# A transformer block on one core: three loads issued behind the copies into the query ring, at the last two attention units, and one rounding of the output weights later in ScalarE's list

## Chip, core and metric

The kernel runs on one core of a Trainium2 chip. The metric is the device time of one execution in microseconds (us). TensorE (PE, with its weight loads as PEld), VectorE (DVE), ScalarE (ACT), GpSimd (POOL) and SyncE (SP, which here only issues DMAs) each work through a list of instructions in order and wait for each other through semaphores.

## What is computed

One block with conditioning (adaLN), sliding-window attention over 2048 tokens with 32 heads of width 16, and a gated FFN, all in float32:

```python
mod = (_silu(c) @ w_mod).reshape(c.shape[0], 6, 1, -1)
sa, ca, ga, sb, cb, gb = (mod[:, 0], mod[:, 1], mod[:, 2], mod[:, 3], mod[:, 4], mod[:, 5])
h = _layernorm(x, axis=-1) * (1 + ca) + sa
x = x + ga * _A_ref(h, A_wqkv, A_wo)       # H = 32, Dh = 16, window of 256 keys
h = _layernorm(x, axis=-1) * (1 + cb) + sb
x = x + gb * _B_ref(h, B_w1, B_w3, B_w2)   # silu(h w1) * (h w3), then w2; F = 1792
```

```python
mask = (idx[:, None] - idx[None, :] >= 0) & (idx[:, None] - idx[None, :] < W)
scores = jnp.where(mask[None, None], scores, -1e9)
p = _softmax(scores, axis=-1)
```

## The kernel before

Products that need more than TensorE's rounded float32 (`F32R`) are made from two parts: a tile is rounded by ScalarE, and VectorE or GpSimd subtracts the rounded part from the tile to get the rest; three products of parts are summed. "Rounding" and "split" below are these two steps.

**Attention** runs in 32 units, one for each group of 4 heads (8 groups) and block of 512 tokens (4 blocks). A unit passes three stages, which for different units lie beside each other in time.

- `unit_a`: the products for queries and keys (L560), rounding and split, and DMAs that place the rows in two tiles that are kept, `ringk` and `ringq` (L579, L581).
- `unit_b`: 16 products of scores (L607, tile `mx`), of each the row maximum over the window on VectorE (L616, into `mt`); the maxima are turned (L622), rounded on ScalarE with the sign changed (`mT`, L626), the rest made on VectorE (L629), and both parts are copied by two DMAs of 8 KB each into two further rows of `ringq` (L633). So a product with `ringq` then subtracts the maximum by itself. These are "the copies" below, two for each unit.
- `unit_c`: the scores again, with the maxima in them (L925, tile `st`, three banks of PSUM), then either a copy (L930), masks on GpSimd (L935) and the exponential (L946), or a merge of two blocks on VectorE (L952), the exponential on ScalarE (L962) and masks on GpSimd; the products with the values (L975, `po`); the result is copied (L982, `os`) and stored (L985, `o_dr`).

**The output projection** starts while the last units still run. Its weights come from `wog` in four loads of 256 KB (L1215), each with a rounding on ScalarE (L1136) and a split on GpSimd or VectorE (L1137). The sums of the softmax are loaded, inverted (`reciprocal`, L1240, between loads L1236 and stores L1241 to `r_dr`); attention's results and the inverses come back in loads of 256 KB each (L1260 from `o_dr`, L1255 from `r_dr`), are multiplied (L1269), rounded (L1264) and split (L1272), and multiplied with the weights (L1283). The input `x` is loaded again in tiles of 256 KB (L1221, `x1a`, `x1b`) and the projection is added to it on VectorE with the sums for the second layernorm (L1153). The FFN follows (L1542, L1638) to the end.

**The order.** From the last units on, the order of all work is a table of numbers, `ORDER`. A negative number is a step of attention, the others are steps of the later phases; the program issues the steps in this order, and each engine gets its instructions, and SyncE its DMAs, in the order in which they come up. An engine whose next instruction waits holds up all that stands behind it on that engine, and this holds for SyncE's queue too. The steps that matter here are -3364 and -3365 (the copies of the last unit but one), -3477 and -3478 (those of the last unit), 14 (the rounding of the second quarter of the output weights), 42 and 43 (loads L1260 and L1255 for the first quarter of the first block), 24 and 26 (loads of `x1a`), 16 and 19 (the loads of the third and fourth quarter of the output weights). Semaphores are set by what the steps read and write, so they follow any order.

```python
    if ORDER:
        order = [ids[i] if i < 0 else sch.ops[i].fn for i in ORDER]
...
    with tc.manual_schedule():
        for fn in first + order:
            fn()
```

Of the kernel before, what the change touches and what calls it, by code (L numbers as in the profile page):

```python
# [272 lines left out]
def us(t):  # L273
# [33 lines left out]
    -3172, -3079, -3329, -3178, -3351, -3359, -3077, -3173, -3330, -3179, -3352, -3360, 31, -3181, -3056, -3076,  # L307
    -3331, -3345, -3164, -3343, -3168, -3075, -3332, -3346, -3344, -3432, 10, 33, -3433, -3252, -3434, -3251,
    -3438, -3435, -3440, -3436, -3439, 32, -3437, -3441, -3175, -3165, -3078, -3357, -3333, -3182, -3335, -3264,
    -3358, -3169, 11, -3081, -3183, -3153, -3170, -3159, -3149, -3180, -3174, 12, -3166, -3334, -3336, -3260,  # L310
    -3265, -3341, -3266, -3189, -3353, -3347, -3261, -3342, -3267, -3354, -3263, -3269, -3150, -3348, -3270,
    -3349, -3258, -3253, -3254, -3355, -3337, -3188, -3350, -3271, -3356, -3338, 34, -3186, -3361, -3255, -3259,
    -3273, -3171, -3362, -3167, -3288, -3284, -3452, -3289, -3290, -3442, 6, 7, 8, 9, -3363, -3285, -3453,
    -3291, -3443, -3082, 13, 42, 43, 26, -3364, -3365, -3287, 14, -3293, -3464, -3185, -3184, -3187, -3472,
    -3274, -3444, -3275, -3465, -3473, -3445, -3458, -3456, -3262, -3272, -3256, -3292, -3459, -3457, -3280,
    -3470, -3294, -3279, -3446, -3295, -3448, -3276, -3190, -3281, -3296, -3471, -3447, -3449, -3454, -3377,
    -3373, -3466, -3378, -3379, -3460, -3302, -3455, -3374, -3380, -3467, -3376, -3462, -3383, -3371, -3468,
    -3268, -3282, -3286, -3277, 44, 15, -3375, -3461, -3450, -3382, -3257, -3283, -3278, -3463, -3469, -3451,
    -3384, -3301, -3299, -3474, -3366, -3367, -3298, -3475, -3372, -3368, -3386, -3401, -3402, -3397, -3403,
    -3297, -3300, 2, -3476, -3398, -3404, -3387, 45, -3400, -3406, 48, 47, -3191, 35, 52, 24, 36, 19, 16, 53,  # L320
    -3477, -3478, -3393, -3392, -3407, -3408, -3388, -3303, -3394, -3389, -3409, -3385, -3369, -3381, -3395,
    -3405, -3390, -3399, 54, 49, 46, 37, 87, -3490, -3491, -3486, 94, -3492, -3487, -3493, -3370, -3489, -3495,
    50, -3391, 80, -3496, -3484, -3415, -3414, -3412, -3479, -3480, -3497, -3499, -3485, -3396, -3481, 55,
    -3514, -3515, -3510, -3411, -3410, -3413, -3516, -3085, 22, -3304, 75, 28, 72, 58, 57, 38, 108, 63, 3, 51,
    73, -3511, -3517, 56, 59, -3513, 17, -3519, 95, 101, 81, -3500, -3506, -3520, -3521, -3505, -3501, -3507,
    -3416, 60, -3522, -3502, 68, 74, 25, 62, 67, 157, 76, -3482, -3498, -3518, -3488, -3508, -3512, -3494,
    -3503, 20, -3509, -3483, -3504, 18, 109, 64, 69, 61, 77, 21, 4, 110, -3417, 23, 29, 39, 162, 156, 88, 89,
    102, 96, 82, -3528, -3527, -3525, -3524, -3523, -3526, 65, -3529, 78, 70, 153, -3530, 79, 137, 116, 103,
    104, 90, 97, 123, 83, 5, 40, 105, 84, 85, 106, 91, 98, 154, 92, 71, 66, 1, 255, 262, 111, 112, 166, 256,
    161, 167, 41, 155, 265, 99, 113, 158, 86, 159, 263, 107, 114, 93, 100, 115, 268, 168, 160, 163, 269, 257,  # L330
    164, 169, 207, 27, 171, 204, 172, 208, 117, 138, 130, 131, 118, 124, 132, 139, 133, 125, 126, 140, 119, 176,
    270, 141, 120, 142, 121, 127, 134, 135, 205, 258, 128, 165, 170, 144, 273, 272, 266, 274, 122, 136, 271,
    143, 129, 183, 197, 198, 184, 190, 191, 192, 282, 288, 199, 185, 177, 267, 275, 209, 212, 213, 206, 147,
    218, 146, 217, 148, 173, 276, 283, 174, 290, 210, 289, 175, 277, 214, 223, 151, 150, 222, 145, 496, 152,
    259, 278, 279, 280, 281, 215, 178, 200, 193, 186, 179, 308, 284, 286, 285, 287, 194, 201, 195, 292, 202,
    293, 187, 188, 294, 180, 211, 291, 219, 216, 220, 196, 297, 309, 306, 299, 295, 316, 189, 203, 300, 181,
    307, 296, 298, 303, 221, 224, 234, 248, 227, 235, 241, 242, 249, 228, 243, 229, 312, 314, 310, 250, 236,
    301, 225, 313, 311, 304, 260, 226, 302, 305, 318, 319, 320, 317, 323, 332, 499, 182, 325, 315, 321, 497,
    327, 251, 237, 230, 244, 359, 447, 335, 341, 149, 448, 454, 457, 451, 252, 324, 264, 403, 326, 253, 336,
    337, 238, 239, 342, 328, 245, 231, 246, 333, 261, 322, 343, 329, 240, 360, 254, 363, 377, 361, 365, 367,  # L340
    364, 330, 458, 404, 338, 366, 362, 405, 344, 369, 345, 331, 247, 452, 406, 378, 368, 408, 449, 407, 409,
    383, 374, 371, 385, 381, 379, 410, 500, 339, 372, 453, 386, 375, 232, 373, 376, 233, 395, 382, 370, 455,
    411, 380, 525, 384, 450, 498, 387, 462, 464, 413, 389, 392, 419, 416, 334, 340, 572, 346, 569, 353, 347,
    412, 388, 456, 390, 391, 526, 348, 527, 459, 393, 394, 401, 465, 414, 422, 415, 478, 460, 466, 529, 531,
    461, 528, 573, 417, 530, 570, 397, 399, 354, 355, 349, 467, 402, 350, 463, 482, 472, 475, 484, 468, 532,
    473, 356, 470, 351, 476, 400, 357, 396, 398, 574, 578, 418, 575, 479, 420, 358, 686, 421, 469, 471, 474,
    483, 576, 477, 687, 533, 541, 535, 480, 507, 490, 352, 683, 429, 534, 423, 536, 481, 577, 571, 485, 491,
    488, 424, 425, 688, 508, 492, 537, 585, 486, 501, 538, 493, 515, 503, 579, 539, 489, 430, 431, 432, 433,
    580, 516, 494, 487, 502, 504, 513, 505, 587, 511, 581, 509, 646, 774, 540, 647, 689, 648, 542, 517, 582,
    523, 519, 586, 649, 651, 588, 495, 514, 426, 654, 512, 427, 510, 605, 589, 593, 583, 599, 596, 603, 434,  # L350
    543, 692, 650, 653, 652, 428, 617, 655, 760, 761, 441, 435, 521, 620, 618, 684, 518, 584, 524, 619, 522,
    520, 591, 594, 656, 685, 442, 436, 597, 621, 592, 600, 590, 595, 690, 604, 693, 598, 701, 607, 622, 601,
    611, 626, 437, 602, 623, 443, 444, 438, 763, 606, 439, 445, 506, 694, 699, 624, 609, 612, 608, 613, 627,
    783, 544, 762, 657, 440, 764, 786, 446, 545, 780, 767, 628, 634, 614, 695, 640, 700, 787, 638, 781, 784,
    696, 610, 765, 768, 641, 625, 546, 629, 635, 639, 547, 770, 702, 632, 636, 630, 707, 697, 703, 548, 637,
    615, 691, 616, 785, 631, 698, 710, 551, 789, 769, 644, 549, 782, 788, 552, 708, 642, 704, 771, 731, 550,
    766, 705, 709, 633, 553, 643, 713, 554, 790, 555, 645, 556, 791, 715, 714, 711, 706, 717, 712, 732, 557,
    716, 734, 733, 719, 563, 718, 860, 735, 721, 720, 558, 725, 559, 722, 560, 561, 723, 728, 562, 658, 861,
    564, 726, 736, 565, 566, 724, 567, 862, 738, 727, 659, 568, 729, 740, 730, 737, 792, 739, 741, 742, 793,
    857, 794, 863, 752, 743, 660, 661, 754, 753, 662, 744, 665, 663, 866, 755, 664, 796, 858, 745, 859, 795,  # L360
    746, 864, 797, 798, 666, 747, 667, 668, 867, 669, 800, 865, 799, 670, 671, 748, 801, 802, 804, 749, 868,
    750, 805, 806, 807, 751, 828, 756, 672, 673, 758, 757, 674, 810, 675, 937, 676, 759, 677, 812, 811, 808,
    803, 814, 809, 829, 813, 831, 830, 816, 938, 815, 832, 818, 817, 678, 869, 679, 819, 680, 681, 820, 772,
    822, 870, 682, 939, 821, 825, 773, 823, 833, 824, 826, 835, 827, 834, 837, 836, 839, 934, 838, 940, 943,
    871, 849, 840, 775, 777, 851, 850, 841, 776, 935, 852, 873, 936, 842, 941, 872, 843, 874, 942, 944, 875,
    844, 778, 877, 876, 945, 779, 845, 878, 881, 846, 879, 847, 1011, 882, 884, 853, 848, 905, 855, 854, 887,
    883, 1014, 856, 1012, 889, 1013, 888, 885, 880, 891, 886, 906, 890, 908, 907, 893, 1015, 892, 909, 895, 894,
# [1414 lines left out]
```

## Time and profile before

| | us |
|---|---|
| three runs | 909.71, 909.88, 911.14 (median 909.88) |
| the profiled execution | 910.79, of which its span is 909.0 |
| TensorE busy in the span | 891.9 |
| VectorE, ScalarE, GpSimd busy | 656.7, 525.8, 555.6 |
| mean granted TensorE clock | 0.994 |

The first attention unit's copies are issued at 75.1 us of the span and the last unit's at 413.7; the FFN's first products (L1542) start at 478.8. A row of the timeline gives start, duration, engine, line, operation, tiles (written <- read), shapes and count, and in brackets how long the engine stood idle before it and for whom; SPq is SyncE's queue, where the duration is that of issuing a DMA. A row of busy times by stretch gives the stretch, its length, the busy time and count of PE, PEld, DVE, ACT and POOL, the granted clock, the share of time in which the DMA engines were busy, and what they moved in GB/s. A wait is attributed by semaphore events, to the one that came last.

### The profile page before, as it was taken

To read this page: it belongs to the slowest core of one execution; us is meant where nothing else is said; L and a number is where in the kernel's file an instruction comes from. 1 tells how busy PE (TensorE), PEld (TensorE's weight loads), DVE (VectorE), ACT (ScalarE), POOL (GpSimd) and SP (SyncE) were. 2 spreads that over 40 slices of the span, in tenths; PEclk is the share of its full clock that TensorE was granted. 3 is DMA by queue.
4 is the path that set the end of the run, shared out by engine and by line. 5 is a ranking of instruction groups with operands and counts; after the bars stand their busy time and mean duration, and the time that the engine had idled before them with its cause. 6 is when DMAs were issued, how large, how long until landed. Compare 5 with 4: busy or idle time off the path is not lost.

```text
span 909.0 us, 18284 instructions
## 1 busy us (share of the span) xinstructions
PE 891.9 (98%) x6011; PEld 726.7 (80%) x6011; DVE 656.7 (72%) x1795; ACT 525.8 (58%) x984; POOL 555.6 (61%) x798
## 2 busy tenths in 40 slices
PE   9999999999999999989999999999999999999998
PEld 5777888887888888857777888888888888888886
DVE  6885888877787878775778768757567665565655
ACT  6437787786778787757588734343374334342330
POOL 3126887787878787866577157886579355434220
PEclk9999999999999999988999999999999999999999
DMA  9524556656655566567866677565272523231102
GB/s 304 185 82 121 144 154 179 161 166 172 186 155 160 154 172 170 151 185 213 257 213 202 202 235 265 169 221 162 63 266 64 172 65 105 74 95 40 47 24 93
DMA packets 126238, 141.98 MB, mean 156 GB/s; under 512 B 61112, under 2 KB 73920, under 8 KB 126144
## 3 DMA queue, kind: packets, MB, share of 16 engines
q1 hardware_dynamic: 126000, 140.82, 51.0%
q8 instruction: 47, 0.77, 0.4%
q14 instruction: 47, 0.39, 0.2%
q10 hardware_dynamic: 144, 0.00, 0.0%
HBM read 85.99 MB, written 34.61 MB: 133 GB/s over the span
## 4 chain that ended last, share of the span: by engine, by line
PE 85%; DVE 4%; DMA 1%; ACT 1%; issue 1%; POOL 1%; SPq 0%; POOLq 0%; DVEq 0%; ACTq 0%
PE st L1542 11%; PE mx L1542 10%; PE st L925 9%; PE po L975 9%; PE pj L560 9%; PE mx L607 8%; PE mx L1638 7%; PE st L1638 6%; PE pj L1542 4%; PE po L1542 3%; PE po L1638 2%; PE pj L1638 2%; PE mx L1283 2%; DMA ringq<-mT 1%; PE st L813 1%
## 5 line engine op out<-in xcount | busy, mean ns | idle before, releaser
L616 DVE CUSTOM_DVE_ANT_0 junk<-mx,mskq 128x320 bf16<-128x320 f32 (+4 forms) x512 | 216.4, 466 | 50.9 <-PE mx L607 49.0
L935 POOL TENSOR_SCALAR_AFFINE_SELECT pt<-pt 128x256 f32<-128x256 f32 x472 | 184.2, 412 | 54.1 <-ACT pt L930 24.4
L607 PE MATMUL mx<-ringk,ringq 96*128 96x320 f32 (+4 forms) x512 | 150.1, 315 | 0.3 <-DMA ringq<-qk 0.2
L560 PE MATMUL pj<-hT,wq 128*128 128x512 f32 x384 | 138.9, 401 | 0.0
L962 ACT ACTIVATE pt<-st 128x512 f32<-128x512 f32 (+1 forms) x216 | 117.3, 572 | 32.6 <-DVE st L952 27.6
L925 PE MATMUL st<-ringq,ringk 98*128 98x256 f32 (+1 forms) x536 | 129.7, 331 | 4.2 <-DMA ringq<-mT 2.1
L1137 POOL TENSOR_TENSOR w<-w,w 128x512 fp32r<-128x512 f32 (+2 forms) x49 | 85.6, 1761 | 52.2 <-ACT w L1136 52.2
L607 PEld LDWEIGHTS mx<-ringk,ringq 96*128 96x128 f32 x512 | 96.4, 191 | 12.3 <-DVE mt L616 1.6
L925 PEld LDWEIGHTS st<-ringq,ringk 98*128 98x128 f32 x536 | 88.8, 192 | 15.3 <-ACT pt L962 4.0
L975 PE MATMUL po<-pt,vS 128*17 128x128 f32 (+1 forms) x2144 | 88.5, 313 | 0.3 <-ACT pt L946 0.3
L560 PEld LDWEIGHTS pj<-hT,wq 128*128 128x128 f32 x384 | 71.8, 190 | 10.3
L975 PEld LDWEIGHTS po<-pt,vS 128*17 128x17 f32 x2144 | 60.8, 98 | 22.4 <-issue 5.0
L952 DVE COPY_PREDICATED st<-later,st 128x256 f32<-128x256 uint8 x152 | 62.1, 426 | 22.0 <-PE st L925 19.9
L1589 POOL TENSOR_TENSOR t<-t,t 128x512 f32<-128x512 f32 x25 | 33.6, 1344 | 65.1 <-DVE t L1577 65.1
L1542 PE MATMUL st<-b,w 128*128 128x512 f32 x270 | 66.9, 390 | 0.2 <-DVE x1a L1643 0.2
L1542 PEld LDWEIGHTS st<-b,w 128*128 128x128 f32 x270 | 50.6, 188 | 11.1 <-DVE x1a L1643 0.7
L946 ACT ACTIVATE pt<-pt 128x512 f32<-128x512 f32 (+1 forms) x96 | 52.5, 587 | 10.6 <-POOL pt L935 10.6
L930 ACT ACTIVATE pt<-st 128x512 f32<-128x512 f32 (+1 forms) x96 | 52.0, 545 | 9.1 <-PE st L925 8.4
L1136 ACT ACTIVATE w<-w 128x512 fp32r<-128x512 f32 (+2 forms) x56 | 42.3, 783 | 17.0 <-DMA w<-wraw 12.0
L1577 DVE TENSOR_TENSOR t<-mx,t 128x512 f32<-128x512 f32 x44 | 30.2, 686 | 28.5 <-PE mx L1542 11.6
L573 POOL TENSOR_TENSOR qk<-qkr,qk 128x512 fp32r<-128x512 f32 x32 | 41.1, 1284 | 14.2 <-ACT qk L569 14.0
L813 PE MATMUL st<-wvh,hT 128*128 128x512 f32 x128 | 44.8, 406 | 1.0 <-DVE hT L474 0.8
(326 smaller groups left out, 1888.5 us busy)
## 6 DMA issues: line engine op xcount, KB each, us to landing
ringq<-qk SPq DMA_DIRECT2D x192, 64.0 KB, 2.1
ringk<-qk SPq DMA_DIRECT2D x96, 128.0 KB, 2.4
o_dr<-os SPq DMA_DIRECT2D x32, 256.0 KB, 2.8
w<-wsum SPq DMA_DIRECT2D x14, 512.0 KB, 4.6
w<-w2g SPq DMA_DIRECT2D x14, 512.0 KB, 4.5
jb<-in_w SPq DMA_DIRECT2D x24, 256.0 KB, 4.9
w<-wraw SPq DMA_DIRECT2D x14, 384.0 KB, 3.8
e<-in_w SPq DMA_DIRECT2D x18, 256.0 KB, 3.1
```

What stands on the lines that cost most here:

```text
L560: nc.tensor.matmul(v["ps"], WQ[g][w][:, n // 3], hTp(i, n // 3, b * BT, BT), start=(n == 0), stop=(n == 3 * KC - 1))
L607: nc.tensor.matmul(v[i][:, :n], both_queries(a, gs), keys(NS, a, (gs + 1) * HP - n, n), start=True, stop=True)
L616: nc.vector.tensor_tensor_reduce(out=junk[:, :n], in0=v[i][:, :n], in1=mskq[:, WK - n:], scale=1.0, scalar=-3e38, op0=ALU.add, op1=ALU.max ...
L813: nc.tensor.matmul(v["ps"], hTp(w, k, t * P, P), i[:, k], start=(n == 0), stop=(n == 3 * KC - 1))
L925: nc.tensor.matmul(piece(v[a, k], a, k, m), keys(NM, a, kb * P, P), queries(a, 4 * b + q, n), start=new, stop=not new or len(here(a, k)) = ...
L935: nc.gpsimd.affine_select(out=out, in_=in_, **w)
L952: nc.vector.copy_predicated(o, later, block(v[a, fk], a, fk, m))
L962: nc.scalar.activation(o, i, AF.Exp, scale=SCALE)
L975: nc.tensor.matmul(po[32 * i:32 * i + DH + 1, q * P:(q + n) * P], vS[:, 4 * b + j, 4 * g + i], piece(pt_of(a, k), a, k, m)[:, h], start=i ...
L1137: either(lambda e: e.tensor_tensor(out=lo(), in0=src(), in1=hi().bitcast(F32), op=ALU.subtract), 0.85, 0.06 + 0.0024 * n, key, kl + kh, kl ...
L1542: nc.tensor.matmul(ps(bk), WT[s, n][w][:, col], BB[t, k][r], start=start and c == 0, stop=stop and c == 5, skip_group_check=True)
L1638: nc.tensor.matmul(ps(bk), tiles[hk + (h,)][:, i * P:(i + 1) * P], w2_of(last, y, f), start=(m == 0), stop=(m == 5))
```

## The change

Only `ORDER` differs. Three loads (42, 43, 26) go behind the copies of the last unit but one, the rounding 14 goes 31 places down the table, and three loads (24, 19, 16) go behind the copies of the last unit. The table is laid out anew over more lines, so that every line below it has a number higher by 3: L633 of before is L636 of the change, and so on. The lines of the table that carry the moves:

```diff
-    -3291, -3443, -3082, 13, 42, 43, 26, -3364, -3365, -3287, 14, -3293, -3464, -3185, -3184, -3187, -3472,
...
-    -3297, -3300, 2, -3476, -3398, -3404, -3387, 45, -3400, -3406, 48, 47, -3191, 35, 52, 24, 36, 19, 16, 53,
-    -3477, -3478, -3393, -3392, -3407, -3408, -3388, -3303, -3394, -3389, -3409, -3385, -3369, -3381, -3395,
...
+    7, 8, 9, -3363, -3285, -3453, -3291, -3443, -3082, 13, -3364, -3365, 42, 43, 26, -3287, -3293, -3464,
...
+    -3292, -3459, -3457, -3280, -3470, -3294, -3279, -3446, -3295, -3448, -3276, -3190, -3281, -3296, 14,
...
+    48, 47, -3191, 35, 52, 36, 53, -3477, -3478, 24, 19, 16, -3393, -3392, -3407, -3408, -3388, -3303,
```

On SyncE, at the copies of the last unit but one, the queue before the change reads (the two copies are the row with `ringq<-mT`; the store and the load of output weights stand ahead of everything here):

```order
L985 DMA o_dr_75<-os 128x512
L1215 DMA wo_7326<-wog 128x512
L1260 DMA qkr<-o_dr_72 128x1x512
L1255 DMA qk_7599<-r_dr_77 128x1x512
L1221 DMA x1a<-in_x 128x512
L633 DMA ringq<-mT 1x16x128 x2
L1255 DMA qk_7818<-r_dr_77 128x1x512
```

and of the change:

```order
L988 DMA o_dr_75<-os 128x512
L1218 DMA wo_7326<-wog 128x512
L636 DMA ringq<-mT 1x16x128 x2
L1263 DMA qkr<-o_dr_72 128x1x512
L1258 DMA qk_7601<-r_dr_77 128x1x512
L1224 DMA x1a<-in_x 128x512
L1258 DMA qk_7818<-r_dr_77 128x1x512
```

The copies have passed three loads of 256 KB; what stands ahead of and behind the six is as it was.

On SyncE, at the copies of the last unit, before the change:

```order
L1260 DMA wq_7824<-o_dr_72 128x1x512
L1221 DMA x1a<-in_x 128x512
L1236 DMA wqr<-o_dr_74 96x1x128
L1215 DMA wo_7326<-wog 128x512 x2
L1255 DMA wq_7830<-r_dr_77 128x1x512
L633 DMA ringq<-mT 1x16x128 x2
L1044 DMA wsum<-jb_7174 128x512
```

and of the change:

```order
L1263 DMA wq_7824<-o_dr_72 128x1x512
L1239 DMA wqr<-o_dr_74 96x1x128
L1258 DMA wq_7827<-r_dr_77 128x1x512
L636 DMA ringq<-mT 1x16x128 x2
L1224 DMA x1a<-in_x 128x512
L1218 DMA wo_7326<-wog 128x512 x2
L1047 DMA wsum<-jb_7174 128x512
```

One load of `x` and two of output weights stood ahead of the copies and now stand right behind them.

On ScalarE, between the two units' `mT`, before the change (the rounding of output weights is the row with `wo`):

```order
L946 ACTIVATE pt<-pt 128x256
L962 ACTIVATE pt<-st 128x512
L1136 ACTIVATE wo_7325<-wo_7326 128x512
L962 ACTIVATE pt<-st 128x512
L930 ACTIVATE pt<-st 128x512
L982 ACTIVATE os<-po 128x512
L930 ACTIVATE pt<-st 128x512
L962 ACTIVATE pt<-st 128x512 x3
```

and of the change:

```order
L949 ACTIVATE pt<-pt 128x256
L965 ACTIVATE pt<-st 128x512 x2
L933 ACTIVATE pt<-st 128x512
L985 ACTIVATE os<-po 128x512
L933 ACTIVATE pt<-st 128x512
L965 ACTIVATE pt<-st 128x512
L1139 ACTIVATE wo_7325<-wo_7326 128x512
L965 ACTIVATE pt<-st 128x512 x2
```

Five activations of attention have passed the rounding. TensorE's, VectorE's and GpSimd's lists hold the same instructions in the same order as before.

197 rows, old and new, of the table ORDER are left out of this document.

## The prediction

> **What bounds the kernel now.** The page comes first: TensorE is busy for 98% of the span and carries 85% of the chain that ended last, so only two things on TensorE can move the time: idle time on the chain, and the clock.
>
> ```profile
> span 909.0 us, 18284 instructions
> PE   9999999999999999989999999999999999999998
> PEclk9999999999999999988999999999999999999999
> PE 85%; DVE 4%; DMA 1%; ACT 1%; issue 1%; POOL 1%; SPq 0%; POOLq 0%; DVEq 0%; ACTq 0%
> ```
>
> The clock digit dips in slices 18 and 19 of 40 (386 to 432 us), and the busy digit of TensorE in slice 18. TensorE's waits, asked next, begin with two reasons whose longest cases lie there:
>
> ```profile
> PE st L925 <- DMA ringq<-mT: 2.1, 2, 1.8
> PE st L925 <- ACT pt L962: 2.0, 2, 1.3
> PE st L1283 <- DVE o L1272: 1.8, 1, 1.8
> ```
>
> The columns are total us, times, longest; the third is a wait in the output projection, behind the change. The timeline of TensorE shows both longest ones, 1.26 and 1.78 us, within five microseconds of each other, in the scores of the last two attention units (the x2 row at 406.16 uses the maxima that the copies bring):
>
> ```profile
> 402.98 0.50 PE L925 MATMUL st<-ringq,ringk 98*128 98x256 f32 x2 [1.26 <-ACT pt L962]
> 406.16 0.98 PE L925 MATMUL st<-ringq,ringk 98*128 98x256 f32 x2 [1.78 <-DMA ringq<-mT]
> ```
>
> Busy time by stretch, cut where the clock changes (length, busy PE, PEld, DVE, ACT, POOL, clock, DMA share, GB/s), shows the price behind them:
>
> ```profile
> 400.10:403.51 3.41, 2.15 (x12) 1.53 (x12) 2.40 (x12) 1.69 (x4) 0.44 (x2) 1.00 0.87 244
> 403.51:406.93 3.42, 1.64 (x6) 1.19 (x6) 1.39 (x6) 1.37 (x3) 3.28 (x9) 0.50 0.92 274
> 406.93:410.34 3.41, 3.41 (x20) 2.30 (x19) 2.04 (x8) 2.15 (x5) 3.30 (x5) 0.50 0.75 235
> 410.34:413.75 3.41, 3.41 (x22) 1.44 (x21) 1.32 (x8) 0.79 (x3) 0.00 (x0) 0.50 0.37 130
> 444.47:447.88 3.41, 2.37 (x10) 1.33 (x9) 2.71 (x4) 2.55 (x6) 1.55 (x2) 1.00 0.86 258
> 475.19:478.60 3.41, 2.20 (x10) 1.83 (x11) 3.38 (x6) 2.00 (x3) 1.17 (x1) 1.00 0.17 66
> ```
>
> After a stretch with 2.15 us busy of 3.41 the clock halves, and it comes back only after 10.24 us. TensorE is busy for 1.64+3.41+3.41 = 8.46 us of these; at full clock that is 4.23.
>
> **Part 1: the copies ahead of three loads.** The issuing queue before the change, and one step of the chain of waits:
>
> ```profile
> 396.28 0.55 SPq L985 DMA_DIRECT2D o_dr<-os  x1
> 396.88 0.45 SPq L1215 DMA_DIRECT2D wo<-wog  x1
> 397.37 0.56 SPq L1260 DMA_DIRECT2D qkr<-o_dr  x1
> 398.04 0.55 SPq L1255 DMA_DIRECT2D qk<-r_dr  x1
> 398.63 0.59 SPq L1221 DMA_DIRECT2D x1a<-in_x  x1
> 399.26 1.20 SPq L633 DMA_DIRECT2D ringq<-mT  x2
> 399.88 6.14 DMA ringq<-mT
> DMA to landing us min/median/max: 1.8/1.8/6.1
> 397.77 0.22 DVE L629 SCALAR_TENSOR_TENSOR mT<-mx,mT 16x128 fp32r<-16x128 f32 x1
> ```
>
> The second 8 KB copy takes 6.14 us from issue to landing, where the median of these copies is 1.8. VectorE made its data at 397.77+0.22 = 397.99. So it can be issued at about 398.3 instead of 399.88. The store and the wo load still stand ahead; ScalarE's row below shows that load landed by 401.82, so the copy lands between 400.1 (398.3+1.8) and about 402.2. TensorE, without the 1.26 us, asks for it at 406.16-1.26-1.78 = 403.1. The 1.78 us wait goes.
>
> The price is on the queue: SyncE now waits at the second copy until 397.99, with the three loads and all later ones behind it, and issues the loads at about 399.2 instead of 397.37. The first taker is GpSimd's multiplication L1269.
>
> ```profile
> 403.00 3.98 POOL L935 TENSOR_SCALAR_AFFINE_SELECT pt<-pt 128x256 f32<-128x256 f32 x10 [3.76 <-ACT pt L962]
> 406.95 1.28 POOL L1269 TENSOR_TENSOR qkr<-qkr,qk 128x512 f32<-128x512 f32 x1
> 401.82 0.63 ACT L1136 ACTIVATE wo<-wo 128x512 fp32r<-128x512 f32 x1 [2.30 <-DMA wo<-wog]
> 402.35 0.58 ACT L962 ACTIVATE pt<-st 128x512 f32<-128x512 f32 x1
> 399.21 0.42 DVE L952 COPY_PREDICATED st<-later,st 128x256 f32<-128x256 uint8 x1
> ```
>
> GpSimd's ten masks will start at about 400.4 (part 2) and end at 404.4. With the worst landing seen, 6.14 us, the loads are there at 405.3. So the new wait costs GpSimd from nothing to 0.9 us, and TensorE nothing, as the masks that TensorE needs next stand ahead of L1269. If that cover went, 0.9 us would reach TensorE.
>
> **Part 2: the rounding behind five activations.** L1136 sat for 2.30 us on its load, and the exponential L962 behind it, whose input VectorE had finished at 399.21+0.42 = 399.63, ran at 402.35. It moves to about 399.7, GpSimd's masks with it, and TensorE's 1.26 us wait for L962 goes. The rounding itself then runs at about 403 with its load landed; its taker, GpSimd's split L1137, stands behind L1269, so it is hidden.
>
> **The engine bound of both.** In the 10.24 us at half clock TensorE needs 4.23 at full clock. VectorE is next:
>
> ```profile
> 403.51:413.75 10.24, 4.75 (x20) 0.50 0.68 213
> ```
>
> (VectorE alone: 4.75 us busy.) So this stretch can shrink to 4.75: 10.24-4.75 = 5.49, and with the 1.26 us before it 6.75 us. By TensorE alone it would be 10.24-4.23+1.26 = 7.27.
>
> **Part 3: three loads behind the last unit's copies.** One x1a and two wo loads leave the queue ahead of the last copies, where the queue had time, and come right behind them.
>
> ```profile
> 413.74 1.18 SPq L633 DMA_DIRECT2D ringq<-mT  x2
> 424.52 0.66 ACT L1136 ACTIVATE wo<-wo 128x512 fp32r<-128x512 f32 x1
> 422.59 0.94 DVE L1240 RECIPROCAL mT<-mT 32x128 f32<-32x128 f32 x1 [0.49 <-DMA mT<-o_dr]
> ```
>
> Their own takers have room: the first is the rounding L1136 at 424.52, over 10 us behind the copies at 413.74, and x1a is taken later, with the projection's sums. The edit's own saving is nothing here: the copies of the last unit had an empty queue already, and TensorE shows no wait for them. What they do is load the wire at its tightest: the reciprocal L1240 already waits for its load, and merges for TensorE stand behind it on VectorE. The DMA stretches:
>
> ```profile
> 399.90:402.00 2.10, 1.83 (x10) 1.20 (x8) 2.10 (x11) 0.18 (x1) 0.00 (x0) 1.00 0.99 277
> 402.00:406.00 4.00, 1.39 (x6) 1.00 (x6) 1.88 (x10) 2.88 (x6) 2.80 (x8) 0.69 0.86 254
> 406.00:409.60 3.60, 3.44 (x19) 2.37 (x20) 1.60 (x6) 1.41 (x3) 3.60 (x6) 0.50 0.78 238
> 409.60:412.20 2.60, 2.60 (x17) 1.56 (x20) 1.67 (x7) 1.23 (x3) 0.63 (x2) 0.50 0.66 225
> 412.20:415.60 3.40, 3.40 (x35) 1.59 (x27) 0.79 (x3) 2.11 (x6) 0.45 (x2) 0.77 0.03 10
> 415.60:422.50 6.90, 6.90 (x83) 5.11 (x83) 4.87 (x8) 6.51 (x13) 6.70 (x14) 1.00 0.84 239
> ```
>
> Up to this load 0.58+1.02+0.86+0.59+0.03+1.65 = 4.73 MB pass in 22.6 us, the moved loads among them in both kernels. At 277 GB/s, the rate with the engines full, they need 17.1 us, so the load can land 5.5 us earlier; at 254, 18.6 us and 4.0 earlier. I take 277, since in the changed kernel the idle 3.4 us at 412 fills up and the DMA engines run full.
>
> **Sum.** The engines allow 6.75 us, the wire 5.5; the smaller holds. From it I take 0.3 for two more hand-offs (0.14 us lie between the copy's landing, 399.88+6.14 = 406.02, and the matmul at 406.16). Gain 5.2 us. After that stretch the chain stays on TensorE to the end, with 1.8 us (at L1283) as its longest wait, and what that wait hangs on comes from attention and moves with it, so I let all of the gain arrive. The profiled execution took 910.79 us (span 909.0 and 1.8 around it) and would take 905.6; the median of the runs is 0.91 lower, so 909.88-5.2 = **904.7**. With the wire at 254 GB/s 906.2, with the engines' bound 903.1, with TensorE's own 902.6.
>
> **Rivals.**
> *The clock halves all the same.* For it: stretches with 2.20 and 2.37 us busy kept the clock, one with 2.15 lost it, so the edge is thin, and the new TensorE may still be paced by VectorE there. Against it: the filled 1.26 us lifts that stretch well over 2.4 busy, and no other slice of the page shows a clock under 9 tenths. Then only the waits go: 1.26+1.78-0.3 = 2.7 us, 907.2.
> The Trainium skill (TensorE: Matmul & The Clock Gate, HAM oscillation — how this bites in real kernels) asks only that TensorE have no idle gap above some 3.4 us; by that rule gaps of 1.26 and 1.78 us did not cost the clock, and removing them would not save it: this rival. The trace speaks against the rule, as the clock fell without a gap over 1.78 us.
>
> *The wire gives less.* At 238 GB/s 4.73 MB take 19.9 us, the load comes 2.7 us earlier, and later loads, such as the one that VectorE waits 1.40 us for in the row below, give some back: gain 1.5 to 2.7, 907.2 to 908.4. For it: rows of 225 to 254 GB/s, though with the queue not full. Against it: 277 where it is.
>
> ```profile
> 431.36 0.72 DVE L1269 TENSOR_TENSOR wq<-wq,wq 128x512 f32<-128x512 f32 x1 [1.40 <-DMA wq<-o_dr]
> ```
>
> *It doesn't do what it says.* The copies still stand behind a 256 KB store and a 256 KB load; if they land after 405, the wait and the clock stay: 909.9. Against it: the wo load had landed by 401.82 with three loads behind it.
>
> *Slower.* At the reciprocal L1240 the three loads (0.79 MB, 3.3 us at 238 GB/s) come ahead of its load; VectorE stands, merges behind it, then TensorE. From a stop of 1.26 us in one 3.41 us stretch the clock falls as above, which costs 1.26 to 3.3 and 8.46-4.23 = 4.23 us, so 5.5 to 7.5 against the 5.2 gained: 910.2 to 912.2. For it: L1240 waits already. Against it: the loads come when the wire was idle.
>
> **Numbers.** Forecast 0.56, clock 0.17, wire 0.14, nothing 0.06, slower 0.07. About 0.2% (1.8 us) is what a measurement can tell from no change; the wire's case lies within it with 0.02 of its 0.14. So faster 0.85, same 0.08, slower 0.07. The range reaches from 902.6 (TensorE's own bound) to 908.4 (the wire's low end) and leaves out the last two cases, 0.13.
>
> **What would show it.** Right: no clock of 0.50 around 403 to 414; L633 at about 2 us to landing; the 1.26 and 1.78 gone from TensorE's waits; L962 ahead of L1136 without 2.30 idle; the 412 us hole in the DMA closed; VectorE's wait at L1240 for mT<-o_dr above 0.49. Wrong: the clock at 0.50 there or further on, a wait of TensorE on L952's merges or on L1137 and L1269, or a copy that lands after 403.

## The result, and the profile after

| | before | change |
|---|---|---|
| median of the runs, us | 910.21 (4 runs, 909.71 to 911.14) | 905.38 (4 runs, 904.83 to 907.24) |
| profiled execution / its span, us | 910.79 / 909.0 | 905.31 / 903.5 |
| ratio, 95% interval | | 0.9945 (0.9928 to 0.9962) |

The change takes 4.8 us off the median. The profiled executions lie 5.5 us apart, and about 0.4 of these is not the change's: the turn of the last unit but one (the `mx<-ident,mt` row that makes its `mT`) stands at 397.04 before and at 396.66 after, ahead of everything that was moved. The trace therefore shows some 5.1 us, where the prediction said 5.2. Measured twice more, on two chips, the change took 4.0 and 3.9 us off the median (the table below), so 5 us is the upper end of what was measured. Three executions far above the others of their kernels (975.64, 979.55 and 1458.08 us) are left out of every median and ratio here.

The page of the change, the lines that answer to those of before:

```profile
span 903.5 us, 18286 instructions
PE   8999999999999999999999999999999999999998
PEclk9999999999999999999999999999999999999999
PE 84%; DVE 3%; DMA 2%; ACT 1%; POOL 1%; issue 1%; SPq 1%; POOLq 0%; DVEq 0%; ACTq 0%
```

The clock's two digits of 8 are gone, and so is TensorE's in slice 18. The wait for the copy and the 1.26 us case have left the list of TensorE's waits between 380 and 500 us (us in total, times, longest):

```profile
PE st L1286 <- DVE o L1275: 1.9, 1, 1.9
PE pj L1545 <- DVE b L1443: 1.3, 1, 1.3
PE st L1419 <- ACT wqr L1405: 1.2, 1, 1.2
PE st L928 <- ACT pt L965: 1.0, 2, 0.5
```

Behind the attention's end stand waits that before had too or that come and go between runs. The line with L965 (L962 of before) is new in its place: two waits of half a microsecond at 420.65 and 421.66, to which the section on the steps comes back.

The timeline of both kernels gives the turns of the last two units, first before, then after:

```profile
397.04 0.28 PE L622 MATMUL mx<-ident,mt 128*16 128x128 f32 x1
413.03 0.38 PE L622 MATMUL mx<-ident,mt 128*16 128x128 f32 x1
```

```profile
396.66 0.28 PE L625 MATMUL mx<-ident,mt 128*16 128x128 f32 x1
406.22 0.28 PE L625 MATMUL mx<-ident,mt 128*16 128x128 f32 x1
```

They lie 15.99 us apart before and 9.56 after: 6.43 us are won between them, within 0.02 of the engines' bound of 6.75 less 0.3. (In the two later profiles of the change they lie 9.64 and 9.60 us apart, so the agreement is closer than the profiles agree with each other.) The distance between these two rows serves below as the measure of the place; it doesn't contain what happens earlier in a run. The busy times of the change by stretch show what ends it now (length, busy PE, PEld, DVE, ACT, POOL, clock, DMA share, GB/s):

```profile
400.10:403.51 3.41, 3.41 (x22) 2.45 (x24) 3.41 (x17) 2.69 (x5) 2.52 (x8) 1.00 0.86 252
403.51:406.93 3.42, 3.42 (x47) 2.04 (x48) 3.00 (x14) 3.03 (x7) 3.42 (x5) 1.00 0.99 300
406.93:410.34 3.41, 3.41 (x55) 2.38 (x46) 2.34 (x5) 3.36 (x8) 3.15 (x8) 1.00 0.55 157
412.20:415.60 3.40, 3.40 (x38) 2.26 (x37) 1.58 (x4) 3.03 (x8) 3.26 (x7) 1.00 1.01 375
```

TensorE has no idle time left here, the clock is whole, and VectorE is busy for 3.41 of 3.41 and 3.00 of 3.42 us: the engine that the prediction named as next. Both engines are full here, so that VectorE and not TensorE sets the pace is argued and not shown. The DMA hole of before at 412 is filled (1.01 of the time busy, 375 GB/s).

### The profile page after: what moved, and what is told of

Same layout as the page of the kernel before. It is cut to its first block, busy times and chain, and to the rows that moved or that the text cites. A ratio compares the mean times of both kernels' runs of the same rounds, so it can differ in the third digit from the quotient of the medians.

```text
span 903.5 us, 18286 instructions
## 1 busy us (share of the span) xinstructions
PE 887.5 (98%) x6011; PEld 723.5 (80%) x6011; DVE 654.2 (72%) x1795; ACT 526.2 (58%) x984; POOL 555.4 (61%) x798
## 4 chain that ended last, share of the span: by engine, by line
PE 84%; DVE 3%; DMA 2%; ACT 1%; POOL 1%; issue 1%; SPq 1%; POOLq 0%; DVEq 0%; ACTq 0%
PE st L1545 11%; PE mx L1545 10%; PE st L928 9%; PE po L978 9%; PE pj L563 9%; PE mx L610 8%; PE mx L1641 7%; PE st L1641 6%; PE pj L1545 4%; PE po L1545 3%; PE po L1641 2%; PE pj L1641 2%; PE st L816 1%; DVE b L1443 1%; POOL xt L747 1%
## 5 line engine op out<-in xcount | busy, mean ns | idle before, releaser
L965 ACT ACTIVATE pt<-st 128x512 f32<-128x512 f32 (+1 forms) x216 | 117.2, 572 | 33.3 <-DVE st L955 27.4
L928 PE MATMUL st<-ringq,ringk 98*128 98x256 f32 (+1 forms) x536 | 128.0, 327 | 2.7 <-ACT pt L965 1.7
L928 PEld LDWEIGHTS st<-ringq,ringk 98*128 98x128 f32 x536 | 87.9, 190 | 13.2 <-ACT pt L965 3.6
L1139 ACT ACTIVATE w<-w 128x512 fp32r<-128x512 f32 (+2 forms) x56 | 42.4, 784 | 18.1 <-DMA w<-wraw 12.8
```

What stands on the lines that cost most here:

```text
L928: nc.tensor.matmul(piece(v[a, k], a, k, m), keys(NM, a, kb * P, P), queries(a, 4 * b + q, n), start=new, stop=not new or len(here(a, k)) = ...
L965: nc.scalar.activation(o, i, AF.Exp, scale=SCALE)
```

## The experiments

Three theories were to be told apart. The first is the prediction's: Part 1 ends the wait for the copy, Part 2 ends the one for the exponential, the clock holds because TensorE is no longer empty, and Part 3 saves nothing by itself. Its rivals: the clock falls for another reason than the two waits; Part 1 alone would do; Part 3 is needed. The runs were made in three groups, each on one chip and beside runs of before on that chip.

| kernel | parts | median, us | before there | ratio | 95% interval |
|---|---|---|---|---|---|
| copies_only | 1 | 907.04 | 910.48 | 0.9966 | 0.9950 to 0.9983 |
| rounding_only | 2 | 910.37 | 910.48 | 0.9998 | 0.9988 to 1.0007 |
| without_last_loads | 1, 2 | 909.67 | 910.48 | 0.9988 | 0.9974 to 1.0002 |
| filler | none, TensorE kept busy | 908.49 | 910.48 | 0.9979 | 0.9969 to 0.9988 |
| change_again | 1, 2, 3 | 907.11 | 911.13 | 0.9957 | 0.9939 to 0.9976 |
| copies_and_last_loads | 1, 3 | 905.80 | 911.13 | 0.9947 | 0.9929 to 0.9965 |
| last_loads_only | 3 | 913.10 | 911.13 | 1.0017 | 1.0002 to 1.0032 |
| x_loads_later | 1, 2, 3, x later | 906.40 | 911.13 | 0.9949 | 0.9933 to 0.9965 |
| change_5 | 1, 2, 3 | 907.20 | 911.08 | 0.9960 | 0.9945 to 0.9974 |
| x_loads_later_5 | 1, 2, 3, x later | 906.88 | 911.08 | 0.9953 | 0.9937 to 0.9968 |

### Part 1 alone

```diff
-    -3291, -3443, -3082, 13, 42, 43, 26, -3364, -3365, -3287, 14, -3293, -3464, -3185, -3184, -3187, -3472,
+    -3291, -3443, -3082, 13, -3364, -3365, 42, 43, 26, -3287, 14, -3293, -3464, -3185, -3184, -3187, -3472,
```

> Only the copies of the last unit but one pass the three loads; the rounding and the last unit's loads stay as before. Theory (each wait costs its own time, and the clock is lost by a 3.41 us stretch that is too empty): the 1.78 us wait for the copy goes, the 1.26 us wait behind the rounding stays, the stretch before 403.5 stays at about 2.15 us busy, so the clock falls as before, perhaps for fewer stretches: 1.8 to 3.5 us faster than before. Rival (the clock falls only through both waits together): with one wait gone the clock holds and 5 to 6 us are gained.

The turns lie 9.99 us apart, 6.0 less than before, and the clock stays at full speed there. The rounding stands where it stood, and yet TensorE no longer waits for the exponential behind it. The timeline of this kernel shows why, and a new wait:

```profile
396.63 0.45 SPq L1215 DMA_DIRECT2D wo<-wog  x1
400.31 0.63 ACT L1136 ACTIVATE wo<-wo 128x512 fp32r<-128x512 f32 x1 [1.08 <-DMA wo<-wog]
408.29 4.70 DMA ringq<-mT
413.12 0.71 PE L925 MATMUL st<-ringq,ringk 98*128 98x256 f32 x3 [1.37 <-DMA ringq<-mT]
```

The rounding ran 3.68 us after its load was issued, where it had been 4.94 (396.88 to 401.82): a load of 256 KB is used 1.3 us sooner when three others no longer follow it at once. (The other kernels in which the rounding waits for this load agree: 5.16 in Part 3 alone and 4.48 in the one with TensorE kept busy, where the three follow at once, and 3.52 in Parts 1 and 3, where they don't.) That took the exponential, GpSimd's masks and TensorE with it. Behind, at 413.12, TensorE waits 1.37 us for the copies of the *last* unit, which took 4.70 us. Before, TensorE was 6 us later there, and nothing showed. The time, 3.4 us less by the medians and 3.1 by the ratio, lies in the theory's range, but not for the theory's reason: the first wait did not stay, and the clock held, as the rival had it. In this profile the clock is lost for one stretch further on (471.40 to 474.81), behind a wait of 1.87 us in the output projection (L1283).

### Part 2 alone

```diff
-    -3291, -3443, -3082, 13, 42, 43, 26, -3364, -3365, -3287, 14, -3293, -3464, -3185, -3184, -3187, -3472,
+    -3291, -3443, -3082, 13, 42, 43, 26, -3364, -3365, -3287, -3293, -3464, -3185, -3184, -3187, -3472,
...
-    -3470, -3294, -3279, -3446, -3295, -3448, -3276, -3190, -3281, -3296, -3471, -3447, -3449, -3454, -3377,
+    -3470, -3294, -3279, -3446, -3295, -3448, -3276, -3190, -3281, -3296, 14, -3471, -3447, -3449, -3454, -3377,
```

> Only the rounding L1136 goes behind the five activations; all DMAs stay as before. Theory: the 1.26 us wait goes, but the copy still lands about 6 us after its issue, so TensorE waits some 2.9 us for it in one piece; the clock falls one stretch later. 0 to 1.5 us faster than before. Rival (the rounding is the main cause, the copy only a follower): 3 us or more faster, and the wait for the copy does not grow.

It does what was said: the first wait goes, the copy still takes 6.07 us, and TensorE, early, waits 3.17 us for it instead of 1.78. The clock falls one stretch later; the time stays.

```profile
400.91 6.07 DMA ringq<-mT
407.12 0.98 PE L925 MATMUL st<-ringq,ringk 98*128 98x256 f32 x2 [3.17 <-DMA ringq<-mT]
```

```profile
403.30:406.71 3.41, 0.65 (x2) 0.20 (x2) 1.42 (x8) 1.36 (x3) 2.92 (x7) 1.00 1.00 256
406.71:410.12 3.41, 3.00 (x18) 2.00 (x18) 1.44 (x5) 0.98 (x3) 2.10 (x3) 0.50 0.86 232
```

### Parts 1 and 2, the last unit's loads where they were

The edit is that of the change without its third part.

```diff
-    48, 47, -3191, 35, 52, 36, 53, -3477, -3478, 24, 19, 16, -3393, -3392, -3407, -3408, -3388, -3303,
+    48, 47, -3191, 35, 52, 24, 36, 19, 16, 53, -3477, -3478, -3393, -3392, -3407, -3408, -3388, -3303,
```

> Copies of the last unit but one ahead of the loads and the rounding later, as in the change, but the loads at the last unit's copies stay where they were. Theory of the prediction (moving the last three loads saves nothing): as fast as the change, 905 plus or minus 0.7, with the wait of VectorE for mT<-o_dr as long as there, since the same bytes pass. Rival (with TensorE some 6 us earlier the last copies need a free queue): TensorE waits 1 us or more for the last unit's copies, and 1.5 to 4 us of the gain go, 906.5 to 909.

The theory fell: of the 5 us about 1 is left, and its interval reaches to no gain at all. The turns lie 9.73 us apart, so the place is as fast as in the change. What it won is lost at once, at the next copies, and at the clock behind them:

```profile
406.99 0.98 SPq L1215 DMA_DIRECT2D wo<-wog  x2
408.67 1.18 SPq L633 DMA_DIRECT2D ringq<-mT  x2
409.32 4.99 DMA ringq<-mT
414.44 0.71 PE L925 MATMUL st<-ringq,ringk 98*128 98x256 f32 x3 [1.78 <-DMA ringq<-mT]
```

```profile
412.67:416.08 3.41, 1.64 (x8) 1.45 (x9) 0.73 (x2) 1.45 (x4) 3.27 (x10) 1.00 0.94 310
416.08:419.49 3.41, 3.41 (x26) 2.02 (x28) 1.70 (x4) 2.61 (x7) 1.13 (x1) 0.50 0.75 217
```

With the loads that Part 3 moves still ahead of it, the two of output weights among them, the second copy takes 4.99 us to land. In the change, with the copies ahead of these three, the pair issued at 406.83 needs about 2.3; the load of `wq` from `r_dr` stands ahead of the copies in both. Of its ten runs the two fastest (905.35 and 907.20) are those with a mean clock of 1.000; seven others, with 0.995 to 0.998, took 908.9 to 911.6.

### Before, with TensorE kept busy

Five products of the identity into a bank that is free there (each is two instructions in the trace) stand ahead of the two waiting steps; nothing uses them, and what the steps wait for stays.

```diff
+        for at_, n in ((-3377, 3), (-3294, 2)):
+            order[ORDER.index(at_):ORDER.index(at_)] = [lambda k=k: warm(k) for k in range(n)]
```

> The order of before, both waits kept; two products of the identity ahead of the product that waits for L962 and three ahead of the one that waits for the copy, into a free bank, so that TensorE is busy while it would wait. Their results are not used. Theory (the clock fell because the stretch was too empty): the clock stays at 1.00 through 403 to 414, and although TensorE does more work the kernel is 2 to 4.2 us faster than before. Rival (the clock fell for another reason, such as a fixed point of time or the kind of work): the clock falls at 403.5 all the same, and the time is that of before or up to 1 us over it.

The busy time by stretch of this kernel:

```profile
400.30:403.70 3.40, 3.40 (x13) 2.02 (x14) 2.56 (x14) 1.95 (x4) 0.70 (x2) 1.00 0.77 238
403.70:407.10 3.40, 3.40 (x14) 1.96 (x13) 1.32 (x6) 1.22 (x3) 3.10 (x10) 1.00 0.96 258
```

The clock holds, and the turns are 13.62 us apart, 2.4 less than before; the median is 2.0 lower. So the two short waits do cause the fall. The mean clocks of all runs say the same: in all 63 executions of before that were timed beside these kernels the mean clock was 0.992 to 0.996, in Parts 2 and 3 alone too, and in the ten of this kernel it was 0.997 to 1.000. The fall is worth 2.0 to 2.4 us, at the low end of what was expected, and by subtraction some 4 of the 6.4 us at this place come from the waits and from what stood behind them.

### Parts 1 and 3, without Part 2

The edit is Part 1's and the last unit's loads as in the change; the rounding stays.

> Both groups of copies ahead of their three loads, the rounding L1136 where it was before. Theory after the first runs (the rounding waited because its load shared the wire with the three loads behind it; with these behind the copies it lands about 1.5 us earlier): the 1.26 us wait is gone without moving the rounding, and the time is that of the change within 0.7 us, 905 to 906. Rival (the moved rounding is needed): some 1.3 us slower than the change, 906.5 to 907, with a wait of TensorE for L962.

905.80 against 907.11 of the change on the same chip, with ratios whose intervals overlap: the moved rounding isn't needed. No wait for the exponential comes back at the place (turns 10.01 us apart), since the load is there in time, as in Part 1 alone.

### Part 3 alone

```diff
-    -3297, -3300, 2, -3476, -3398, -3404, -3387, 45, -3400, -3406, 48, 47, -3191, 35, 52, 24, 36, 19, 16, 53,
-    -3477, -3478, -3393, -3392, -3407, -3408, -3388, -3303, -3394, -3389, -3409, -3385, -3369, -3381, -3395,
+    -3297, -3300, 2, -3476, -3398, -3404, -3387, 45, -3400, -3406, 48, 47, -3191, 35, 52, 36, 53,
+    -3477, -3478, 24, 19, 16, -3393, -3392, -3407, -3408, -3388, -3303, -3394, -3389, -3409, -3385, -3369, -3381, -3395,
```

> Only the last unit's copies pass their three loads. Theory (those copies had an empty queue as long as TensorE was late): the time of before, 910.4 plus or minus 0.7, both waits and the fallen clock as before. Rival (the move is good or bad by itself, through the wire behind 413 us): 1 to 3 us faster or slower.

Slower by 2.0 us by the medians, and 1.5 by the ratio, as the rival had it. VectorE's waits between 400 and 440 us have the price that the slower rival of the prediction saw coming at L1240, 2.5 us where before had 0.49, and TensorE's timeline has two waits behind it that before had not:

```profile
DVE mT L1240 <- DMA mT<-o_dr: 2.5, 1, 2.5
```

```profile
428.57 0.50 PE L925 MATMUL st<-ringq,ringk 98*128 98x256 f32 x2 [0.32 <-ACT pt L962]
429.58 0.62 PE L925 MATMUL st<-ringq,ringk 98*128 98x256 f32 x3 [0.51 <-ACT pt L962]
```

TensorE loses no clock behind these two, so the slower rival's chain went only half its way. The last scores of attention end 32.4 us after the first turn, where before had 30.9; the two waits are 0.83 us of these 1.6, and the rest is not put down to anything. The same three loads cost up to 2 us without Part 1 and win with it: from 0.9966 (Part 1) to 0.9947 (1 and 3) and from 0.9988 (1 and 2) to 0.9945, 0.9957 and 0.9960 (the change, three times). The first pair's intervals overlap, and each pair was measured on different chips, against before on each. What carries the reading is the wait for the last copies, which both kernels that have Part 1 without Part 3 show and no kernel with Parts 1 and 3 does.

### The change again, and with the loads of x later

The variant puts the loads of `x` 26 and 28 behind id 155 and 24 behind 25, later in the table, to take 0.79 MB off the wire ahead of the reciprocal's load.

```diff
-    -3291, -3443, -3082, 13, -3364, -3365, 42, 43, 26, -3287, -3293, -3464,
+    -3291, -3443, -3082, 13, -3364, -3365, 42, 43, -3287, -3293, -3464,
...
-    -3477, -3478, 24, 19, 16,
+    -3477, -3478, 19, 16,
...
-    -3085, 22, -3304, 75, 28, 72,
+    -3085, 22, -3304, 75, 72,
...
-    74, 25, 62,
+    74, 25, 24, 62,
...
-    41, 155, 265,
+    41, 155, 26, 28, 265,
```

> The change itself once more, for comparison on the same chip: 905.4 plus or minus 0.7, about 5 us faster than before.

> The change, with three loads of x tiles that are added late (tiles 2, 4 and 6) taken from behind the copies at 400, from behind the last copies and from 412 to behind the fourth x tile at about 420 (tile 2) and to about 438 (tiles 4 and 6). 0.79 MB less pass before VectorE's reciprocal L1243, whose wait for its load was 3.63 us. Theory (the wire gives back about 1 us of the gain there): that wait falls below 2 us, TensorE's two waits of 0.47 and 0.50 us for L965 go, 0.7 to 1.3 us faster than the change, about 904.4. Rival (the loads collide later, with the FFN's first weights, or TensorE is held by other things there): as fast as the change or up to 1 us slower.

The change again missed its expectation: 907.11 is 4.0 us under before, not 5. In its profile the clock is lost for one stretch behind the attention (473.23 to 476.64), after a wait of 1.86 us in the output projection (L1286).

The reciprocal's wait shrinks as meant, from 3.56 us in the change again to 2.05 in the variant:

```profile
421.13 0.94 DVE L1243 RECIPROCAL mT<-mT 32x128 f32<-32x128 f32 x1 [3.56 <-DMA qkr<-o_dr]
```

```profile
419.50 0.94 DVE L1243 RECIPROCAL mT<-mT 32x128 f32<-32x128 f32 x1 [2.05 <-DMA mT<-o_dr]
```

Both of TensorE's waits go with it, and the last scores of attention (L928) come 24.16 us after the first turn instead of 25.48. VectorE then waits 2.7 us for another load in the variant (`qk<-o_dr`, at L1272), and the medians are 0.7 us apart with intervals that overlap. Both kernels were timed once more, with more rounds:

> The change, in five rounds beside the next kernel: 5 us faster than before, ratio 0.9945 plus or minus 0.0015.

> The change with the three x loads (tiles 2, 4 and 6) later, in five rounds. In one profile the attention's last scores came 1.3 us earlier after the turn than in the change's. Theory (the wire's give-back reaches the end): 0.7 to 1.3 us faster than the change. Rival (what is won at the merges is lost behind them, as VectorE's multiplication L1272 now waits 2.7 us for its load): within 0.4 us of the change.

0.9960 and 0.9953, with medians 0.3 us apart: the second pair doesn't separate them either, as the rival had it, and the change is again nearer to 4 than to 5 us. That less wire time ahead of the reciprocal shortens its wait is shown; that it makes the kernel faster is not. No kernel of these is shown to beat the change.

## Why the prediction was right, step by step

**The copy and its wait: right, the landing later.** The copies were issued at 397.27 and 397.94, a little earlier than the predicted 398.3, and TensorE did not wait. The landing took longer than said. The source view of the copies' line in the change, 380 to 420 us, has as its last line:

```profile
DMA to landing us min/median/max: 2.3/2.3/4.6
```

The prediction took between 1.8 us and a landing at 402.2 at the latest, and the pair was there at 401.9 (397.27 + 4.6), near that upper bound, so the sign "about 2 us to landing" was not met; TensorE's products with it ran at 402.39. The cover was half a microsecond: a little later, and a wait would have come back, though the rival's own mark, a landing after 405, was 3 us away. The price on GpSimd did not come: its multiplication started at 404.60 without a wait.

**The 1.26 us wait: right that it goes, wrong about what ends it.** The prediction gave it to Part 2. Part 1 ends it already, by letting the rounding's load land sooner, and Part 2 on its own gains nothing (0.9998). The step that failed is to take the rounding's 2.30 us on its load for a time that Part 1 leaves as it is: the load's landing was taken as fixed, though Part 1 moves three loads that share the wire with it.

**The clock: right at this place, not everywhere.** It held, and the filler shows why it fell: emptiness from waits of 1.26 and 1.78 us. The rival that it halves all the same is refuted for this place. Further on, which the prediction named as a sign of being wrong too, it did halve for one stretch in both later profiles of the change (from 473.23 and from 454.44, behind waits of 1.86 and 2.06 us); the first profile was spared. The Trainium skill (TensorE: Matmul & The Clock Gate, HAM oscillation — how this bites in real kernels) asks for no idle gap above some 3.4 us; the traces disagree, since the fall came without such a gap and went when the two shorter ones were filled. In the stretches shown, TensorE was busy for 0.65 us of 3.41 (Part 2 alone), 1.64 (Parts 1 and 2) and 2.15 (before) ahead of a fall; 2.20 and 2.37, in before, were not followed by one. That looks like an edge near 2.2 us, but the other traces don't bear it out. The change again lost the clock behind the first row here, and the second timing of the variant with `x` later kept it behind the second, with the same products and the same wait of TensorE (1.86 and 1.87 us):

```profile
469.82:473.23 3.41, 1.55 (x7) 1.00 (x6) 3.41 (x5) 2.01 (x4) 1.12 (x1) 1.00 0.60 193
468.43:471.84 3.41, 1.54 (x8) 0.96 (x6) 3.41 (x4) 2.00 (x4) 1.52 (x1) 1.00 0.71 210
```

So filling the stretch saved the clock at this place, but the busy time of a stretch alone doesn't say whether the clock falls behind it, and what else decides is open.

**The engines' bound: right in size.** 6.43 us were won between the turns, and VectorE is busy for all of 400.10 to 403.51, as is TensorE.

**Part 3, whose "own saving is nothing": wrong.** The prediction looked for a wait at the last unit's copies in the profile of *before*, found none, and put it at nothing. With TensorE 6 us earlier the same copies are late: 1.4 us in Part 1 alone, 1.8 us and a fall of the clock with Parts 1 and 2. The prediction asked what GpSimd would find late next, and did not ask it for the copies of the next unit. The change came out right because it holds the part that was priced at nothing.

**The wire: the sum right, the term mis-sized.** The prediction let the load for the reciprocal land 5.5 us earlier and let this bound the gain. The timeline of before and of the change, the issue and the use:

```profile
418.95 0.73 SPq L1236 DMA_DIRECT2D mT<-o_dr  x1
422.59 0.94 DVE L1240 RECIPROCAL mT<-mT 32x128 f32<-32x128 f32 x1 [0.49 <-DMA mT<-o_dr]
```

```profile
413.00 0.73 SPq L1239 DMA_DIRECT2D mT<-o_dr  x1
418.71 0.94 DVE L1243 RECIPROCAL mT<-mT 32x128 f32<-32x128 f32 x1 [3.63 <-DMA r_dr<-wqr]
```

The load was *issued* 5.95 us earlier, 5.6 without the 0.4 of the run. But from issue to use it took 5.71 us instead of 3.64, in a stretch where the DMA engines had no free time (412.20 to 415.60 above), so the reciprocal ran 3.9 us earlier, 3.5 without the 0.4. (Which of several loads of those microseconds came last isn't settled: the row names another one, the change again a third, the variant this one.) The mean rate from 399.5 to the reciprocal was 259 GB/s, below the 277 assumed, as the hole moved to 407 to 410 (157 GB/s). That is the prediction's second case, 254 GB/s with a load 4.0 us earlier, and not the 238 of the rival "the wire gives less"; the price of that case, 906.2, did not follow either.

A gain bounded by that would have been 3.5, and the kernel got 5.1: the minimum of the two bounds was the wrong way to join them. TensorE does not stand until the load comes; only what is queued behind the reciprocal on VectorE does. The timeline of the change shows this path. The last scores ahead of VectorE's two merges are done at 418.12, the merges come right behind the reciprocal (418.71 + 0.94 = 419.65), and ScalarE stands for them for 2.85 us:

```profile
417.62 0.50 PE L928 MATMUL st<-ringq,ringk 98*128 98x512 f32 x1
419.58 0.72 DVE L955 COPY_PREDICATED st<-later,st 128x256 f32<-128x256 uint8 x2
420.00 0.60 ACT L965 ACTIVATE pt<-st 128x512 f32<-128x512 f32 x1 [2.85 <-DVE st L955]
420.50 0.62 ACT L1139 ACTIVATE wo<-wo 128x512 fp32r<-128x512 f32 x1
421.02 0.59 ACT L965 ACTIVATE pt<-st 128x512 f32<-128x512 f32 x1
```

and TensorE's rows behind it:

```profile
420.65 0.50 PE L928 MATMUL st<-ringq,ringk 98*128 98x256 f32 x2 [0.47 <-ACT pt L965]
421.66 0.74 PE L928 MATMUL st<-ringq,ringk 98*128 98x256 f32 x4 [0.50 <-ACT pt L965]
```

These two waits are 0.97 of the 1.3 us that separate the 6.43 won at the place from the 5.1 at the end; the other 0.3 is not put down to anything. The second of them, 0.50, is about what the rounding of output weights (L1139) takes that ScalarE runs between the two exponentials, from 420.50 to 421.02; no run moves that one. So the sum that held is the engines' bound less the toll of a late load. That it met the predicted number of the wire is chance.

**What stays open.** Parts 1 and 2 (0.9988) came out behind Part 1 alone (0.9966), on one chip, with intervals that just overlap. In the former's profile TensorE also waits 1.4 us for a mask of GpSimd (`po<-pt` for L935) and loses a stretch of clock; whether that belongs to the moved rounding or to where the clock happened to fall in that execution was not separated. No run's time shows Part 2 to gain anything. At the place itself it may be worth some 0.3 us: the turns lie 9.99 and 10.01 us apart in the two kernels with Part 1 and without Part 2, and 9.56 to 9.76 in the six profiles with both.

## What to carry to other kernels

In a queue that issues in order, put the few kilobytes that an engine waits for ahead of bulk loads, at *every* such place near the one mended: an engine that is made earlier meets the next small transfer earlier, and a wait that isn't in the old profile is in the new one. Test the parts together as well as alone, since a part that costs 2 us by itself can be what lets the other pay. Two short waits close together can cost more than their sum, so read the granted clock by stretch behind them before adding them up, in more than one profile; and when a load is moved, ask which loads ahead of it share its wire and will land at another time too.

## What the hardware showed that was not expected

- The clock falls without a long gap: waits of 1.26 and 1.78 us within some five microseconds brought it to half for 10.24 us, three stretches of 3.41, though TensorE was busy for all of the last two. In other executions one stretch was lost (416.08 to 419.49 in Parts 1 and 2) or two (406.71 to 413.53 in Part 2 alone). The same wait of 1.86 or 1.87 us in the output projection, in a stretch with as little busy time (1.55 and 1.54 us), cost the clock in one profile and not in another (the two rows in the section on the steps).
- Runs of one kernel differ by whether such stretches are lost: the runs of Parts 1 and 2 spread over 6.3 us (905.35 to 911.60), and the fastest are those with a whole clock. It is not the clock alone: in the second timing of the variant with `x` later a run of 909.51 had a mean clock of 1.000 and one of 904.04 had 0.999. One profile of such a kernel can mislead by several microseconds, which is as large as this change.
- A load that was issued earlier takes longer when more is issued behind it: 4.48 to 5.16 us from issue to use in three kernels with three loads of 256 KB right after it, 3.52 and 3.68 in two with the two copies of 8 KB in between.
